# Useless 512-column matmuls in TensorE's waits during the softmax of a one-token GQA decode block

## The chip, the cores and the metric

One core of one Trainium2 chip. The metric is device time of one execution in microseconds (us), the median over several executions. Executions of one kernel scatter here by about 0.2%, so differences under some 1.5 us in single runs mean little, and I then read the trace and not the total.

## The reference, cut to what matters

```python
mod = (_silu(c) @ w_mod).reshape(8, 6, 1, 512)         # sa, ca, ga, sb, cb, gb
h = _layernorm(x) * (1 + ca) + sa                      # x: 8 x 1 x 512
# attention: 8 batches, 32 query heads, 8 KV heads, 8192 keys, head size 128, bf16
q = (h @ wq) ...
p = softmax(q @ k_cache.T * 128 ** -0.5)
x = x + ga * ((p @ v_cache) @ wo)
h = _layernorm(x) * (1 + cb) + sb
x = x + gb * (relu(h @ w1 + b1) ** 2 @ w2 + b2)        # w1: 512 x 1792
```

K and V together are 268 MB, and each byte is used once. The whole kernel reads 284 MB (283.66 on the page, part 3).

## The kernel before

K and V come in 64 units of 4 MiB, each with two KV heads of one batch: for each of the eight batches four units of K, then four of V. A ring of four slots in SBUF holds them. A slot is loaded again as soon as TensorE has read it.

```python
units = [(kv, b, p) for b in range(B) for kv in "kv" for p in range(NP)]   # NP = 4
...
    loaded[n] = dma("sync", s_ring[s], lambda e: e.dma_start(slot(s), src), dep)  # dep: slot released
```

A batch begins with its K phase. TensorE transposes 128 key tiles per unit, 32 at a time, VectorE and ScalarE copy them out of PSUM, and TensorE multiplies them by the queries of all heads. The scores stand in PSUM banks 0 to 3. The softmax follows. It is a chain of small steps that goes back and forth between the engines, and TensorE waits in four places, marked here A to D:

```python
t = op("vector", lambda e: e.tensor_reduce(m1[:], m4[:], AX.X, ALU.max), maxes)
t = op("vector", lambda e: e.tensor_scalar(Dm[:], Qmask[:], m1[:, 0:1], None, ALU.mult), [t, k_all], "vecP")
T_ps = bank(7)[:, 0:4]                                                           # A
t = op("tensor", lambda e: e.matmul(T_ps, R4[:], Dm[:]), [t, stg_free[3]])       # maximum, transposed
t = op("vector", lambda e: e.tensor_reduce(mq[:], T_ps, AX.X, ALU.max), [t])
k_neg = op("vector", lambda e: e.tensor_scalar(negm[:], mq[:], -inv_sqrt, None, ALU.mult), [t])
exps = []                                                                        # B
... # four exponentials on ScalarE; 64 transposes of P on TensorE; copies into Pm
t = op("vector", lambda e: e.tensor_reduce(rs1[:], rs4[:], AX.X, ALU.add))
t = op("vector", lambda e: e.tensor_scalar(rhs_r[:], R4m[:], rs1[:, 0:1], None, ALU.mult), [t, k_all], "vecP")
tot_ps = bank(3)[:, 0:32]                                                        # C
t = op("tensor", lambda e: e.matmul(tot_ps, ONES[:, :], rhs_r[:]), [t])          # row sums
k_rinv = op("vector", lambda e: e.reciprocal(rinv[:], tot_ps), [t], "vecP")      # D
```

The V phase has four units of 32 matmuls with 512 columns each, in four column groups of the array, then a copy, four small matmuls and a scaling by `rinv`. For the last batch this code stands apart. Between its V units it already projects with `wo`, and it loads the last quarter of `wo`, then `w1` and `w2`, behind the last V. A few 128-column fillers of the same kind as in the change (`pe_fill`) stand there already.

## Time and profile before

| what | value | read from |
|---|---|---|
| time | 671.87 us median of 3 (671.45 to 672.91) | the runs |
| busy: TensorE matmul, VectorE, ScalarE | 72%, 45%, 35% of the span | page, part 1 |
| load queue | 98.7% of 16 engines' span | page, part 3 |
| period of a batch | 77.7 us, that is 33.55 MB at 432 GB/s | chain of waits |
| mean granted TensorE clock | 0.862 | span and clock of the core |

The page of the kernel before, parts 2 and 3: TensorE's granted clock, the DMA share (tenths, in 40 slices of 16.8 us), the rate in each slice, then the queue of the loads and the queue that fetches instructions.

```profile
PEclk9999986899859977799868988699757997589979
DMA  9999999999999999999999999999999999999995
GB/s 374 435 419 426 430 431 432 430 430 434 432 432 430 428 436 432 434 430 432 432 430 434 428 432 430 434 434 434 430 426 434 432 436 430 426 436 430 438 393 209
...
q1 hardware_dynamic: 12612, 283.65, 98.7%
q8 instruction: 13, 0.21, 0.1%
```

The DMA row says what bounds the kernel: in every slice but the last the digit is 9, so the DMA engines are busy for 90% or more of it. The rate is 432 GB/s over whole batches; single slices read up to 438. The clock row shows the thing that the change goes after: the clock falls once or twice in every batch, to digits of 5 to 7.

The groups of instructions: the V matmuls (L564). The columns after the bar are busy us, mean ns of one, then TensorE's idle time just before them and what ended most of it.

```profile
L564 PE MATMUL PS<-ring,Pm 128*32 128x512 bf16 x992 | 85.2, 504 | 62.7 <-DMA ring<-in_A_v_cache_dram 58.3
```

TensorE waits 58 us in all for V to arrive (58.3, in 14 waits). In the V phases of the first seven batches it is ahead of the loads.

The timeline of the kernel before, from the softmax of the last batch to the end, TensorE's lines only, with cuts. The columns are start, duration, engine and line, operation, count, and in brackets the idle time before it and its releaser. L511 is the matmul of the maximum, L525 the transposes of P, L544 the row sums, L564 the V units, L645 the last projection by `wo`, L682 the matmuls with `w1`, L699 those with `w2`; L431 are fillers that were there before.

```profile
628.86 0.18 PE L511 MATMUL PS<-Dm,R 128*128 128x4 bf16 x1 [1.26 <-DVE Dm L509]
...
630.29 2.65 PE L525 MATMUL PS<-IDENT,P_sb 128*64 128x128 bf16 x64 [1.25 <-ACT P_sb L516]
...
633.93 0.41 PE L544 MATMUL PS<-rhs_r,ONES 128*128 128x32 f32 x2 [0.99 <-DVE rhs_r L542]
...
634.88 3.02 PE L564 MATMUL PS<-ring,Pm 128*32 128x512 bf16 x32 [0.54 <-DVE rinv L545]
...
638.89 3.59 PE L564 MATMUL PS<-ring,Pm 128*32 128x512 bf16 x32
...
657.77 1.15 PE L645 MATMUL PS<-oTn,wo_sb 128*128 128x64 bf16 x32 [0.29 <-DVE oTn L640]
...
660.68 0.94 PE L431 MATMUL PS<-IDENT 128*128 128x128 bf16 x14
...
661.87 3.55 PE L682 MATMUL PS<-hbT,ring 128*128 128x64 bf16 x56 [0.25 <-DVE hbT L675]
...
665.55 1.48 PE L699 MATMUL PS<-ring,hidT 128*8 128x256 bf16 x24
```

The four waits A to D last 1.26, 1.25, 0.99 and 0.54 us (in the other batches the third is 0.85 or 0.86 and the rest are the same). After them the clock is down (0.50 in the stretch from 636 to 642 us): two V units take 3.02 and 3.59 us, where a warm one takes 1.9 (1.91 in the first batch, at a clock of 1.00). From the first V unit to the start of L645 the trace has no wait of TensorE for a load.

### The profile page before, as it was taken

How to read it: one execution, taken by the hardware profiler on the slowest of the kernel's cores; microseconds unless marked ns; L12 is line 12 of the kernel's file. 1: busy time of each engine (PE TensorE's matmuls, PEld its weight loads, DVE VectorE, ACT ScalarE, POOL GpSimd, SP SyncE). 2: the span in 40 equal slices, each digit the busy share in tenths (PEclk: the TensorE clock that was granted, in tenths of full speed). 3: DMA queues.
4: the chain of work that ended last, by engine and by line, in shares of the span. 5: the costliest groups of instructions: out<-in, count | busy, mean ns of one | idle time of the engine just before them, and what ended most of it. 6: DMA issues, size and time to landing. Idle time of an engine off the chain costs nothing.

```text
span 670.8 us, 15938 instructions
## 1 busy us (share of the span) xinstructions
PE 481.1 (72%) x7366; PEld 345.6 (52%) x7366; DVE 300.3 (45%) x568; ACT 235.3 (35%) x281; POOL 17.0 (3%) x67
## 2 busy tenths in 40 slices
PE   2289843997459964698629973699647986399787
PEld 2277621875137731576318751477316753187445
DVE  2146721567116751466216661267414673166612
ACT  2045600465006630365105650166203661056500
POOL 7200000000000000000000000000000000000000
PEclk9999986899859977799868988699757997589979
DMA  9999999999999999999999999999999999999995
GB/s 374 435 419 426 430 431 432 430 430 434 432 432 430 428 436 432 434 430 432 432 430 434 428 432 430 434 434 434 430 426 434 432 436 430 426 436 430 438 393 209
DMA packets 12682, 283.96 MB, mean 423 GB/s; under 512 B 1234, under 2 KB 2291, under 8 KB 3956
## 3 DMA queue, kind: packets, MB, share of 16 engines
q1 hardware_dynamic: 12612, 283.65, 98.7%
q8 instruction: 13, 0.21, 0.1%
q14 instruction: 9, 0.07, 0.0%
q10 hardware_dynamic: 48, 0.02, 0.0%
HBM read 283.66 MB, written 0.01 MB: 423 GB/s over the span
## 4 chain that ended last, share of the span: by engine, by line
PE 57%; DMA 35%; DVE 4%; ACT 2%; issue 1%
PE PS L439 36%; DMA ring<-in_A_k_cache_dram 33%; PE PS L454 9%; PE PS L564 4%; PE PS L525 3%; DMA ring<-in_w_mod_dram 2%; ACT KTb L444 1%; ACT P_sb L516 1%; DVE m L459 1%; DVE Pm L538 1%; PE PS L544 1%; PE PS L483 1%; PE PS L682 0%; DVE rinv L545 0%; PE PS L386 0%
## 5 line engine op out<-in xcount | busy, mean ns | idle before, releaser
L444 ACT ACTIVATE KTb<-PS 128x1024 bf16<-128x1024 bf16 x192 | 196.7, 1024 | 369.9 <-PE PS L439 369.9
L439 PE MATMUL PS<-IDENT,ring 128*128 128x128 bf16 x4096 | 268.1, 228 | 45.7 <-DMA ring<-in_A_k_cache_dram 36.5
L439 PEld LDWEIGHTS PS<-IDENT,ring 128*128 128x128 bf16 x4096 | 247.5, 103 | 94.0 <-DMA ring<-in_A_k_cache_dram 38.0
L446 DVE COPY KTb<-PS 128x1024 bf16<-128x1024 bf16 x320 | 210.2, 688 | 145.3 <-PE PS L439 143.3
L564 PE MATMUL PS<-ring,Pm 128*32 128x512 bf16 x992 | 85.2, 504 | 62.7 <-DMA ring<-in_A_v_cache_dram 58.3
L573 DVE CAST O_sb<-PS 128x512 bf16<-128x512 f32 x31 | 21.4, 692 | 144.1 <-PE PS L564 144.1
L454 PE MATMUL PS<-KTb,Qb 128*32 128x512 bf16 x1024 | 78.8, 384 | 4.5 <-ACT KTb L444 4.5
L564 PEld LDWEIGHTS PS<-ring,Pm 128*32 128x32 bf16 x992 | 30.1, 118 | 99.4 <-DMA ring<-in_A_v_cache_dram 59.6
L525 PE MATMUL PS<-IDENT,P_sb 128*64 128x128 bf16 x512 | 25.2, 269 | 10.4 <-ACT P_sb L516 10.0
L577 PEld LDWEIGHTS PS<-SEL,O_sb 128*128 128x128 bf16 x124 | 5.2, 98 | 45.5 <-DVE O_sb L573 45.5
L516 ACT ACTIVATE P_sb<-PS,negm 128x512 bf16<-128x512 f32 x32 | 21.6, 686 | 18.9 <-DVE negm L513 18.9
L525 PEld LDWEIGHTS PS<-IDENT,P_sb 128*64 128x64 bf16 x512 | 21.0, 140 | 13.5 <-ACT P_sb L516 13.2
L538 DVE COPY Pm<-PS 64x512 bf16<-64x512 bf16 x48 | 20.1, 421 | 16.2 <-PE PS L525 15.1
L454 PEld LDWEIGHTS PS<-KTb,Qb 128*32 128x32 bf16 x1024 | 15.4, 94 | 21.0 <-ACT KTb L444 8.5
L577 PE MATMUL PS<-SEL,O_sb 128*128 128x8 bf16 x124 | 8.0, 170 | 24.8 <-DVE O_sb L573 24.8
L459 DVE TENSOR_REDUCE m<-PS 128x1 f32<-128x512 f32 x32 | 22.1, 689 | 6.6 <-PE PS L454 6.6
L535 ACT ACTIVATE Pm<-PS 64x512 bf16<-64x512 bf16 x16 | 9.5, 593 | 5.5 <-PE PS L525 5.4
L580 DVE TENSOR_TENSOR oTn<-PS,rinv 128x8 bf16<-128x8 f32 x31 | 6.0, 193 | 10.9 <-PE PS L577 10.9
L398 PE MATMUL PS<-haT,ring 128*128 128x8 bf16 x128 | 3.7, 168 | 9.1 <-DMA ring<-in_A_wq_dram 6.4
L672 ACT ACTIVATE std<-PS,epst 128x8 f32<-128x8 f32 x1 | 0.3, 268 | 26.0 <-PE PS L670 26.0
L544 PE MATMUL PS<-rhs_r,ONES 128*128 128x32 f32 x16 | 4.2, 349 | 7.0 <-DVE rhs_r L542 7.0
L511 PE MATMUL PS<-Dm,R 128*128 128x4 bf16 x8 | 1.4, 178 | 10.1 <-DVE Dm L509 10.1
(114 smaller groups left out, 105.7 us busy)
## 6 DMA issues: line engine op xcount, KB each, us to landing
ring<-in_A_k_cache_dram SPq DMA_DIRECT2D x32, 4096.0 KB, 35.2
ring<-in_A_v_cache_dram SPq DMA_DIRECT2D x31, 4096.0 KB, 27.8
ring<-in_A_wq_dram SPq DMA_DIRECT2D x1, 4096.0 KB, 19.8
ring<-in_w_mod_dram SPq DMA_DIRECT2D x1, 3072.0 KB, 10.5
wo_sb<-in_A_wo_dram SPq DMA_DIRECT2D x1, 3072.0 KB, 45.2
ring<-in_A_v_cache_dram SPq DMA_DIRECT2D x1, 2048.0 KB, 22.4
ring<-in_B_w_dram SPq DMA_DIRECT2D x1, 1536.0 KB, 14.7
ring<-in_B_w_dram SPq DMA_DIRECT2D x1, 1344.0 KB, 21.8
```

Of the source, the lines that this page charges most:

```text
L439: t = op("tensor", lambda e, j=j, i=i: e.matmul(STG[j][:, i, :], src[:, 32 * k + 8 * j + i, :], IDENT[:, :], is_transpose=True), [loaded[n ...
L444: stg_free[j] = op("scalar", lambda e, j=j, dst=dst: e.activation(dst, STG[j], ACT.Copy), [t], "scaP")
L446: stg_free[j] = op("vector", lambda e, j=j, dst=dst: e.tensor_copy(dst, STG[j]), [t], "vecP")
L454: t = op("tensor", lambda e, hf=hf, q=q, rhs=rhs: e.matmul(PS[32 * q:32 * (q + 1), k, :], Qb[:, 2 * p + hf, :], rhs, start=(p == 0 and hf ...
L459: return op("vector", lambda e: e.tensor_reduce(m4[:, k:k + 1], bank(k), AX.X, ALU.max), [t])
L516: exps.append(op("scalar", lambda e, k=k: e.activation(P_sb[:, k, :], bank(k), ACT.Exp, bias=negm[:, 0:1], scale=inv_sqrt, accum_out=rs4[: ...
L525: t = op("tensor", lambda e, k=k, i=i, hf=hf, src=src: e.matmul(STG[k][64 * hf:64 * (hf + 1), i, :], src, IDENT[:, :], is_transpose=True, ...
L538: done.append(op("vector", lambda e, dst=dst, frm=frm: e.tensor_copy(dst, frm), [t, k_pm], "vecP"))
L544: t = op("tensor", lambda e: e.matmul(tot_ps, ONES[:, :], rhs_r[:]), [t])
L564: t = op("tensor", lambda e, p=p, m=m, cg=cg, vt=vt, Obank=Obank: e.matmul(Obank[32 * cg:32 * (cg + 1), :], lhs[:, p, 32 * m:32 * m + 32], ...
L573: t = op("vector", lambda e, osb=osb, Obank=Obank: e.tensor_copy(osb, Obank), [t], "vecP")
L577: t = op("tensor", lambda e, i=i, osb=osb, oT_ps=oT_ps: e.matmul(oT_ps, osb[:, i * 128:(i + 1) * 128], SEL[:, i, :], start=(i == 0), stop= ...
```

## The change

Its intent: fill the four waits with plain matmuls whose results nobody uses, in the hope that TensorE then keeps its clock of 1.00 and runs the V phase of each batch at full speed. The banks written (4 and 1) are free at that moment.

```diff
+        def pe_stream(n, at):
+            rhs = IDENT[:, :].unsqueeze(1).to_broadcast([128, 4, 128])
+            for _ in range(n):
+                op("tensor", lambda e: e.matmul(
+                    bank(at).rearrange("p (a r) -> p a r", a=4), IDENT[:, :], rhs))
...
             t = op("vector", ... Dm ...)
+            pe_stream(5, 4)                      # A
             T_ps = bank(7)[:, 0:4]
...
             k_neg = op("vector", ... negm ...)
+            pe_stream(5, 4)                      # B
             exps = []
...
             t = op("vector", ... rhs_r ...)
+            pe_stream(3, 1)                      # C
             tot_ps = bank(3)[:, 0:32]
             t = op("tensor", lambda e: e.matmul(tot_ps, ONES[:, :], rhs_r[:]), [t])
             k_rinv = op("vector", lambda e: e.reciprocal(rinv[:], tot_ps), [t], "vecP")
+            pe_stream(2, 1)                      # D
```

## The prediction

> **What bounds the kernel now.** The DMA engines. The utilisation slices show DMA at 90% or more in 39 of 40, and the queue table gives the load queue 98.7% of the 16 engines' span. Stretches of 10 us from 20 to 640 move 413 to 442 GB/s, mostly 429 to 436. [...] In the chain of waits the batches repeat every 77.7 us; eight loads of 4 MiB in 77.7 us are 432 GB/s. The K phase of a batch takes TensorE 16 x 2.44 = 39.0 us, as long as four loads. The softmax adds about 8 us, and the V phase, where TensorE is faster than the loads, pays it back: its waits for V loads sum to 58 us, some 7 us a batch. A load lands a median 35.2 (K) or 27.8 (V) us after its issue; alone it would take 9.7, so the queue always holds more work. TensorE's lag never starves DMA.
>
> **What the change does.** It adds 120 matmuls of 512 columns (15 in each of 8 batches), with no new semaphore and no copy; it removes nothing. One such stream costs, estimated from V units of 32 matmuls in groups of four (1.94 us at full clock, 3.59 at half), 0.24 us warm and 0.45 cold. The gaps of TensorE before the four consumers (timeline, waits): 1.26 us before the maximum transpose, 1.25 before the P transposes, about 0.9 before the row-sum matmul, 0.54 before V. Warm fillers take 1.2, 1.2, 0.7 and 0.5: they fit, with 0 to 0.3 us of delay per batch. The clock is still 1.00 when the softmax starts.
>
> What it buys is clock. In the last batch the granted clock is 1.00 up to 634 us and then 0.50 from 636 to 642; the first two V units take 3.02 and 3.59 us instead of 1.94. [...] With fillers both should run near 1.94, at least the first: 1 to 2.7 us off TensorE's chain per batch.
>
> **How much is on the critical path.** In batches 1 to 7 nothing: TensorE arrives earlier at V and waits longer for V. Only after the last softmax is TensorE the last chain. There it gains up to 2.7 us by the second V unit, but loads cut it short: the last piece of wo lands at about 656.4 (needed at 657.8), the main part of w2 at about 664.5 (needed at 665.55). They queue behind a saturated DMA and don't move. So at most about 1 us reaches the end; I count 0.8 us, less a little for fillers in the way and for a new cold spell where TensorE waits for wo.
>
> **Predicted time: 671.2 us, range 669.9 to 672.7.** Faster by over 2%: 1%; within 2%: 98%; slower by over 2%: 1%.
>
> **What would show it right or wrong.** Right: batch period still 77.7 us; DMA slices unchanged; waits of the V matmuls for V loads up by some 5 to 15 us; the first V unit after a softmax at 1.9 to 2.2 us with clock 1.00; TensorE busy up by 20 to 30 us before what warm V saves; P transposes at most 0.3 us later after the last scores. Wrong: a batch period off 77.7, a DMA slice below 90% in the middle, or the last V units still at half clock.
>
> **What would make it wrong.** Fillers running cold (0.45 us each) would delay the softmax by up to 3 us, harmless but in the last batch. A clock drop moved onto the last w1 matmuls (3.4 us warm) would cost up to 3 us. Either stays under 1%.

671.87 us, less the 0.8 us counted at the end, with a little given back for fillers in the way and a new cold spell, is 671.2. The 9.7 us of a load alone is an estimate: 4 MiB at the 432 GB/s of a batch.

## More of the kernel before

A run is called fast or slow by its state. Only the verdicts of repeated runs use that; a single run has the state "unknown".

TensorE runs the eight batches as a loop: its instruction stream exists once and is repeated. The other engines' streams are unrolled.

## The result, and the profile after

| | before | after |
|---|---|---|
| median | 671.71 us (4 runs, 671.45 to 672.91) | 672.50 us (4 runs, 671.75 to 672.71) |
| profiled span | 670.8 us | 670.6 us |
| mean granted clock | 0.862 | 0.885 |

The ratio is 1.0006, with a 95% interval of 0.9989 to 1.0024: the same. A ratio is the mean time of one kernel's fast runs over that of the other's of the same rounds, so it is not quite the ratio of the medians.

The page of the changed kernel, the same lines as above.

```profile
PEclk9997997899869996699859997699967998699996
DMA  9999999999999999999999999999999999999995
GB/s 372 434 419 428 430 432 430 430 432 430 434 432 429 432 434 432 434 426 434 432 432 434 424 432 432 436 436 422 434 432 432 436 430 426 434 432 436 436 389 217
...
q1 hardware_dynamic: 12612, 283.65, 98.8%
q8 instruction: 13, 0.21, 0.1%
```

The DMA rows have not changed. The clock row has; it still falls in each batch, but later, where TensorE waits for V (to 0.50 in the seventh batch, below). The groups, V matmuls and fillers (L436):

```profile
L574 PE MATMUL PS<-ring,Pm 128*32 128x512 bf16 x992 | 81.0, 484 | 63.8 <-DMA ring<-in_A_v_cache_dram 62.9
...
L436 PE MATMUL PS<-IDENT 128*128 128x512 bf16 x120 | 31.3, 380 | 0.0
```

The V matmuls are busy for 4.2 us less, and TensorE waits 4.6 us longer for V. (The 380 ns of one filler come from matmuls that overlap. Five take 1.25 us together.) The two figures don't belong to the same batches. Of the 4.2 us, 3.3 fall in the last batch, whose V units are shown below. In the first seven, V is busy for 75.3 us, against 76.1 before. There the first V units took 6.0 us less in all (13.4 against 19.4), and the third ones took 5.0 us more (23.6 against 18.6). The third unit of the seventh batch in the timeline, before and then after:

```profile
565.70 1.91 PE L564 MATMUL PS<-ring,Pm 128*32 128x512 bf16 x32 [1.11 <-DMA ring<-in_A_v_cache_dram]
```

```profile
565.85 3.36 PE L574 MATMUL PS<-ring,Pm 128*32 128x512 bf16 x32 [3.85 <-DMA ring<-in_A_v_cache_dram]
```

TensorE comes to the third unit earlier and waits for the same load: 25.9 us in the seven batches, against 16.3. Around the end of this longer wait the clock falls (in the seventh batch to 0.50 at about 566.2 us). So the cold spell has moved from the first unit to the third, where the wait for the fourth load takes it up: that wait shrank from 42.0 to 37.0 us.

What the clock did around one softmax: a stretch of the profile from the last scores to the second V unit of the seventh batch. The columns are length, busy us of each engine with instruction counts, then the granted clock, the DMA share and GB/s. First the kernel before:

```profile
545.00:562.00 17.00, 11.66 (x170) 6.80 (x171) 9.09 (x22) 6.35 (x13) 0.00 (x0) 0.80 1.00 432
```

The same stretch of the changed kernel:

```profile
545.00:562.00 17.00, 14.15 (x210) 7.29 (x202) 9.22 (x22) 6.01 (x12) 0.00 (x0) 1.00 1.00 432
```

The clock goes from 0.80 to 1.00, and the loads run at 432 GB/s in both.

The timeline of the changed kernel, the last batch, the lines that answer to those of before (L518 maximum, L533 transposes of P, L574 V, L655 `wo`, L692 `w1`, L709 `w2`):

```profile
628.41 0.18 PE L518 MATMUL PS<-Dm,R 128*128 128x4 bf16 x1
...
629.84 2.64 PE L533 MATMUL PS<-IDENT,P_sb 128*64 128x128 bf16 x64 [0.15 <-ACT P_sb L524]
...
634.43 1.91 PE L574 MATMUL PS<-ring,Pm 128*32 128x512 bf16 x32
...
637.32 1.91 PE L574 MATMUL PS<-ring,Pm 128*32 128x512 bf16 x32
...
656.63 1.86 PE L655 MATMUL PS<-oTn,wo_sb 128*128 128x64 bf16 x32 [2.32 <-DMA wo_sb<-in_A_wo_dram]
...
660.47 1.65 PE L431 MATMUL PS<-IDENT 128*128 128x128 bf16 x14
...
661.91 3.52 PE L692 MATMUL PS<-hbT,ring 128*128 128x64 bf16 x56
...
665.60 1.48 PE L709 MATMUL PS<-ring,hidT 128*8 128x256 bf16 x24 [0.16 <-DVE hidT L700]
```

Both V units now take 1.91 us; the second ends 3.2 us earlier than before (639.2 against 642.5). Then TensorE has to wait 2.32 us for the last piece of `wo`. It starts the projection 1.14 us earlier than before, at 656.63, but at a lower clock: it fell during the wait, and is 0.50 from 655 us until past 662. The projection takes 1.86 us where it took 1.15, and the 14 old fillers 1.65 where they took 0.94. At the first matmul with `w1` the two kernels stand level again, 661.91 against 661.87.

### The profile page after: what moved, and what is told of

Its sections match the earlier page's. It is cut to its first block, busy times and chain, and to the rows that moved or that the text cites. A ratio compares the mean times of both kernels' runs of the same rounds, so it can differ in the third digit from the quotient of the medians.

```text
span 670.6 us, 16178 instructions
## 1 busy us (share of the span) xinstructions
PE 498.8 (74%) x7486; PEld 345.4 (52%) x7486; DVE 299.3 (45%) x568; ACT 235.1 (35%) x281; POOL 17.0 (3%) x67
## 4 chain that ended last, share of the span: by engine, by line
PE 51%; DMA 40%; DVE 5%; ACT 2%; issue 1%; SPq 0%; ACTq 0%
PE PS L445 36%; DMA ring<-in_A_k_cache_dram 35%; PE PS L460 9%; DMA wo_sb<-in_A_wo_dram 4%; DVE Pm L546 3%; PE PS L574 2%; ACT KTb L450 1%; DMA KTb<-in_A_x_dram 1%; ACT P_sb L524 1%; DVE m L465 1%; PE PS L533 1%; PE PS L436 0%; PE PS L692 0%; PE PS L553 0%; PE PS L431 0%
## 5 line engine op out<-in xcount | busy, mean ns | idle before, releaser
L574 PE MATMUL PS<-ring,Pm 128*32 128x512 bf16 x992 | 81.0, 484 | 63.8 <-DMA ring<-in_A_v_cache_dram 62.9
L574 PEld LDWEIGHTS PS<-ring,Pm 128*32 128x32 bf16 x992 | 29.1, 114 | 100.8 <-DMA ring<-in_A_v_cache_dram 64.1
L436 PE MATMUL PS<-IDENT 128*128 128x512 bf16 x120 | 31.3, 380 | 0.0
L587 PEld LDWEIGHTS PS<-SEL,O_sb 128*128 128x128 bf16 x124 | 5.2, 98 | 45.1 <-DVE O_sb L583 45.1
L546 DVE COPY Pm<-PS 64x512 bf16<-64x512 bf16 x48 | 19.5, 419 | 13.4 <-PE PS L533 12.4
L533 PE MATMUL PS<-IDENT,P_sb 128*64 128x128 bf16 x512 | 20.4, 222 | 2.0 <-ACT P_sb L524 1.2
L533 PEld LDWEIGHTS PS<-IDENT,P_sb 128*64 128x64 bf16 x512 | 15.2, 109 | 9.8 <-ACT P_sb L524 9.8
L436 PEld LDWEIGHTS PS<-IDENT 128*128 128x128 bf16 x120 | 9.9, 103 | 10.8 <-issue 3.4
```

What stands on the lines that cost most here:

```text
L436: op("tensor", lambda e: e.matmul(bank(at).rearrange("p (a r) -> p a r", a=4), IDENT[:, :], rhs))
L533: t = op("tensor", lambda e, k=k, i=i, hf=hf, src=src: e.matmul(STG[k][64 * hf:64 * (hf + 1), i, :], src, IDENT[:, :], is_transpose=True, ...
L546: done.append(op("vector", lambda e, dst=dst, frm=frm: e.tensor_copy(dst, frm), [t, k_pm], "vecP"))
L574: t = op("tensor", lambda e, p=p, m=m, cg=cg, vt=vt, Obank=Obank: e.matmul(Obank[32 * cg:32 * (cg + 1), :], lhs[:, p, 32 * m:32 * m + 32], ...
L587: t = op("tensor", lambda e, i=i, osb=osb, oT_ps=oT_ps: e.matmul(oT_ps, osb[:, i * 128:(i + 1) * 128], SEL[:, i, :], start=(i == 0), stop= ...
```

## The experiments

The theory: the loads bind. The fillers keep the clock through the softmax, what they save becomes waiting for V, and at the end waiting for `wo`. The main rival: TensorE's chain binds, and the fillers cost in the softmax what they give back in V, so that the net is zero. A zero result fits both; the experiments must break the tie. Twelve kernels ran, and all passed the comparison with the reference.

### 1. The changed kernel again, and 2. with fillers in the wait for wo

> The changed kernel once more, unaltered, so that the tail variant can be set against it in the same rounds. The theory (loads bind; the fillers' gain is absorbed by waits for V and, at the end, for the last piece of wo) expects 671.5 to 672.7 us and a ratio to before of 0.999 to 1.002. A rival, that the fillers cost time in the softmax which their warm clock pays back, expects the same ratio; this run does not separate them.

```diff
                     t = direct(112, 128, 3, False, True)
+                    pe_stream(9, 7)
                     t = op("vector", ... oTn_p ... rinv_p ...)
```

> The changed kernel with nine more 512-column fillers where TensorE waits 2.3 us for the last piece of wo in the final batch. Theory (the wait for wo cooled the clock, and the cold projection, transposes and fillers then gave back what was left of the gain): the projection by wo still starts near 656.6 us, limited by the load, but takes 1.15 instead of 1.86 us; the first w1 matmul starts near 660.8 instead of 661.9; the w2 matmuls start near 664.5, when w2 lands; span 669.5 to 669.9, about 0.8 to 1.0 us shorter than the changed kernel, a ratio of 0.9985 to it. Rival (the tail is bound by the loads of w1 and w2 alone): no change of the span, first w2 matmul still at 665.6.

Measured in five rounds together with the kernel before (672.26 us): the changed kernel again 672.29 us (671.66 to 672.56, ratio 1.0001, interval 0.9987 to 1.0014), the tail variant 671.72 us (671.44 to 672.52, ratio 0.9997, interval 0.9983 to 1.0011). The tail variant's timeline, from the wait for `wo`:

```profile
654.16 2.11 PE L436 MATMUL PS<-IDENT 128*128 128x512 bf16 x9
...
656.64 1.13 PE L656 MATMUL PS<-oTn,wo_sb 128*128 128x64 bf16 x32 [0.38 <-DMA wo_sb<-in_A_wo_dram]
...
660.73 3.55 PE L693 MATMUL PS<-hbT,ring 128*128 128x64 bf16 x56 [0.25 <-DVE hbT L686]
...
664.71 1.48 PE L710 MATMUL PS<-ring,hidT 128*8 128x256 bf16 x24 [0.43 <-DMA ring<-in_B_w_dram]
```

In this profile each step fell where the theory put it. The projection starts when `wo` lands and takes 1.13 us; `w1` starts at 660.73; then the tail runs into the landing of `w2`, at 664.7. The span was 669.7 us against 670.6, as expected. The totals are 0.6 us apart in the median, and the intervals overlap, so this is no version that is shown to beat both; 0.9 us of 670 is about what one execution differs from the next. The expected ratio of 0.9985 to the changed kernel was missed: the two ratios above make it 0.9996. One reason is to be seen in the repeated run of the changed kernel: there the projection happened to run warm (1.14 us) and only the fillers after it were cold, `w1` started at 661.26, and the span was 670.1 us.

### 3. and 4. More fillers: 25 and 60 instead of 5 in wait A

```diff
-            pe_stream(5, 4)                      # A
+            pe_stream(25, 4)                     # or 60
```

> The changed kernel with 25 instead of 5 fillers before the maximum transpose: 20 more at 0.24 us, so each of the eight softmaxes ends 4.8 us later. Theory (loads bind): batch period still 77.7 us, waits of the V matmuls for V loads down by about 4 us a batch; in the last batch the 4 us of waits for V and wo swallow it: 671.5 to 673 us. Rival (TensorE's chain binds, and gain and cost of the fillers happened to cancel): 8 x 4.8 = 38 us more, about 710 us.

> As the last one with 60 fillers: 13.2 us later in each softmax, 106 us of added TensorE work in all. Theory: batch period still 77.7 us, because TensorE has some 19 us of waiting in a batch and a load issued at the end of a V unit has more than 13 us of others queued ahead; only the last softmax shows, with 13.2 less the 4 us of waits and 1.2 of a cold spell that no longer occurs: about 8.3 us more than the changed kernel, 679.5 to 682 us. Rival (TensorE's chain binds): about 778 us.

With 25: 673.95 us (672.02 to 674.22), ratio 1.0016, interval 1.0000 to 1.0033. The batch period is still 77.7 us, though TensorE has 8 x 4.4 = 35 us more to do (25 fillers took 5.50 us in the chain of waits, so 4.4 us for twenty). The rival's 710 us is out. The waits for V fell from 62.9 to 45.1 us, 2.5 us a batch and not the 4 that I expected; a good part of the rest came out of the third V units, which now started after a short wait or none: they took 14.0 us in the first seven batches, against 23.6. I had expected 671.5 to 673 us. The median is 1 us above that. In the profiled execution (674.22 us) a cold spell fell between the V units of the last batch: its third V unit took 2.94 us instead of 1.91, and the first piece of the fourth 1.90 instead of 1.05.

With 60: 705.63 us. Neither 680 nor 778. The period grew to about 80 us, so the theory as I had put it missed something. The page of that run, the instruction queue:

```profile
q8 instruction: 76, 1.25, 0.7%
```

The instruction queue carried 76 packets instead of 13, and the chain of waits had waits of 1.6 to 4.4 us before the K phases and of 5.8 us before the last V phase, with no releaser but "issue". So two causes were mixed in this run: a late softmax, and instructions fetched again and again. Experiments 5 and 9 to 10 look at each alone. How the 33 us divide between them stays open: the delay of 5 is 8.7 us a softmax, and 55 more fillers at 0.22 us are about 12. From the second batch to the seventh no V unit waited for its load in this run, so TensorE's slack was used up.

### 5. A late softmax without one more instruction on TensorE

The kernel before, with twelve useless reductions on VectorE ahead of wait A.

```diff
+            for _ in range(12):
+                t = op("vector", lambda e: e.tensor_reduce(std2[:, 0:1], bank(0), AX.X, ALU.max), [t])
             t = op("vector", ... Dm ...)
```

> The kernel before, with no fillers, and twelve useless reductions of 0.69 us on VectorE before the mask of each softmax: each softmax ends 8.3 us later, and TensorE gets no instruction more, so that nothing of the 60-filler run's extra instruction fetching can come in. Theory (loads bind, a batch has more TensorE waiting than that, and the queue holds loads for longer): batch period 77.7 us still; only the last softmax shows, for by then no waits are left in the kernel before: 6 to 10 us in all, 678 to 682 us. Rival (every softmax is on the chain): 8 x 8.3 = 66 us, about 738 us. Second rival (the 60-filler run was slow because the delay starved the loads): batch period over 79 us and the slices of the DMA below 90% here as well.

An earlier try of this, without the dependency between the reductions, was a race.

Measured: 682.65 us (680.13 to 682.96), ratio 1.0150, interval 1.0128 to 1.0172. In the chain of waits a reduction took 0.725 us from start to start, so 8.7 us were added to each softmax, 70 us in all; about 10 arrived at the end (11.0 between the medians). The K phases start at these times (chain of waits, first 64 transposes of a batch):

```profile
118.53 5.81 PE PS L439 x64
...
196.24 6.20 PE PS L439 x64
...
273.97 6.56 PE PS L439 x64
...
351.68 5.31 PE PS L439 x64
...
429.39 5.69 PE PS L439 x64
...
507.84 5.72 PE PS L439 x64
...
586.52 5.64 PE PS L439 x64
```

Four periods of 77.7 us, as before, then 78.5 and 78.7. The last K phase of the kernel before (chain of waits):

```profile
585.14 6.59 PE PS L439 x64
```

Seven softmaxes that were 8.7 us late cost 1.4 us at the start of the last K phase (586.52 against 585.14), and the last one cost the rest. This is the proof that the softmax of the first seven batches is not on the chain, and why nothing that is saved there can come out. The slack is nearly used up by then, as the two last periods show. The DMA slices stay at 9 up to the tail, so the second rival, loads starved by the delay, is out at 8.7 us. The median is 0.65 us over the range that I had given; the 1.4 us of the two last periods cover it.

### 6. and 7. The loads taken away: half a slot for each K and V unit

From the fifth unit on only half of a slot is loaded and the other half keeps old data. The result is wrong, though the comparison with the reference did not notice it. The same edit in both kernels:

```diff
-                loaded[n] = dma("sync", s_ring[s], lambda e: e.dma_start(slot(s), src), dep)
+                z = UNIT if n < NSLOT else UNIT // 2
+                loaded[n] = dma("sync", s_ring[s], lambda e: e.dma_start(RING[:, s, 0:z], src[:, 0:z]), dep)
```

> The kernel before with the loads of K and V cut to half a slot from the fifth on (the other half keeps old data; the result is wrong on purpose): the DMA engines have 124 MB less to move and TensorE's chain binds. Theory: batch period down to 60 to 65 us (39.0 for K, 8 for the softmax, 12 to 18 for V), 535 to 580 us in all; the first V units after a softmax still partly at half clock.

> The changed kernel with the same halved loads (wrong on purpose). Theory: here the fillers are worth what they save on TensorE, 1 to 4 us a batch, 8 to 30 us in all, a ratio of 0.95 to 0.985 to the halved kernel before; batch period 58.5 to 59.5 us. Rival (the fillers cost in the softmax what they give back in V): ratio to the halved kernel before 0.995 to 1.005.

Measured, three rounds on the same chip: halved kernel before 557.68 us (555.28 to 558.23; one execution of 568.46 at a clock of 0.927 counts as slow and is left out of the ratio), halved changed kernel 550.98 us (550.72 to 551.05). Ratios to the same runs of the unhalved kernel before are 0.8280 and 0.8201, so the fillers give a ratio of 0.8201 / 0.8280 = 0.990, or 6.7 us between the medians (6.1 if the slow execution is left out of them too). The two intervals, 0.8261 to 0.8299 and 0.8187 to 0.8215, don't overlap. The rival expected 0.995 to 1.005. With the loads out of the way the same fifteen fillers pay. (Of the 7.2 us between the two profiled executions, about 1.5 were there before the first filler: the first matmul of a maximum starts at 82.12 us in the one and at 80.66 in the other.)

They pay less than the 8 to 30 us that I expected. Where it comes from: the V units of the sixth batch in the halved kernel before (timeline),

```profile
394.90 3.60 PE L565 MATMUL PS<-ring,Pm 128*32 128x512 bf16 x32 [0.54 <-DVE rinv L546]
...
399.50 3.60 PE L565 MATMUL PS<-ring,Pm 128*32 128x512 bf16 x32
...
404.11 3.58 PE L565 MATMUL PS<-ring,Pm 128*32 128x512 bf16 x32
```

and in the halved changed kernel:

```profile
395.86 1.91 PE L575 MATMUL PS<-ring,Pm 128*32 128x512 bf16 x32
...
398.75 1.91 PE L575 MATMUL PS<-ring,Pm 128*32 128x512 bf16 x32
...
401.65 1.91 PE L575 MATMUL PS<-ring,Pm 128*32 128x512 bf16 x32
```

In three of the eight batches the halved kernel before ran V units cold; in the other five its V units stayed warm without help (1.87 to 1.94 us each in the chain of waits). And in the halved changed kernel six of the seven later K phases began cold: their first 64 transposes took 5.0 to 5.4 us instead of 3.73. In the halved kernel before only one of the seven did, and its periods without a cold spell, 60.9 to 61.0 us, are shorter than any with fillers. The fillers moved part of the cold spell from V to the next K, and what they gain comes from the batches that they keep from the long cold spells (two periods of 66.05 and 63.99 us without them). The cold K start is 1.6 us of the difference between the period, 61.6 to 61.9 us, and the 58.5 to 59.5 that I expected; another 1.0 us is a wait at the loop's start, which I had not counted. What the fillers do beyond the mean is to make the time steady: four executions within 0.33 us, against 3 us without them, or 13 us if the slow one is counted.

### 8. Transposes as fillers

```diff
-                op("tensor", lambda e: e.matmul(bank(at).rearrange(...), IDENT[:, :], rhs))
+                for a in range(4):
+                    op("tensor", lambda e, a=a: e.matmul(
+                        bankb(at)[:, 128 * a:128 * (a + 1)], IDENT[:, :], IDENT[:, :], is_transpose=True))
```

> The changed kernel with each 512-column filler replaced by four 128-column transposes, the same stream of columns but no plain matmul. If transposes don't count as activity for the clock[...], the clock after a softmax falls as in the kernel before: the stretch from 625 to 640 us has a mean granted clock of about 0.85 and the first V unit of a batch takes 3 us or more in most batches. If they count, the clock is 1.00 there and the unit takes 1.9 to 2.0 us. Time 671 to 674 us either way, since the loads bind.

Measured: 689.66 us in one run. The time is a miss, and it has nothing to do with the clock (experiments 9 and 10). For the clock the run is good. The stretch from the first fillers through the first V unit of the seventh batch, and that unit in the timeline:

```profile
559.00:569.00 10.00, 9.23 (x167) 6.50 (x167) 4.82 (x16) 3.97 (x10) 0.00 (x0) 1.00 1.02 437
```

```profile
566.88 1.91 PE L575 MATMUL PS<-ring,Pm 128*32 128x512 bf16 x32
```

The stretch for the test, 625 to 640 us, no longer fits, because this run is 17 us longer; the stretch above is its equal one batch earlier. In all of the first seven batches the unit took 1.9 us, as with plain matmuls; in the kernel before four of the first seven took 3.23 to 3.58. (In the eighth batch a wait of 6.03 us put down to "issue" stands before the unit, and it is cold, 3.63 us.) In this kernel transposes held the clock as well as matmuls did: 1.00 in the stretch above and in the one of the changed kernel. The K phases of the kernel before show it without any filler: the last one begins at 585.14 us at a clock of 0.50, TensorE does nothing but transposes until 591.66, and from about 591.2 us on, after some 6 us, the clock is 1.00. The "plain" in the change is not what makes it work.

### 9. and 10. Instructions alone: 45 and 20 tiny matmuls where TensorE waits for K

```diff
+                    if not lastb and p == NP - 1:
+                        for _ in range(45):      # or 20
+                            op("tensor", lambda e: e.matmul(bank(7)[:, 0:8], IDENT[:, :], IDENT[:, 0:8]))
```

> The changed kernel with 45 useless matmuls of 8 columns at the end of each V phase but the last, where TensorE waits about 5 us for K anyway: as many instructions more in TensorE's loop as in the run with transposes as fillers (45 matmuls and 45 weight loads), but hardly any time. Theory (the two slow filler runs were slow because TensorE's loop body outgrew what it keeps, and was fetched anew for every batch): instruction queue at 60 to 76 packets instead of 13, waits put down to issue of 2 to 6 us at the loop's branches, 684 to 692 us. Rival (those runs were slow through the extra stream or the transposes): 13 packets and 671.5 to 673 us.

> The same with 20 matmuls, as many instructions as the run with 25 fillers, which still fetched only 13 packets. Theory: 13 packets, 671.5 to 673.5 us. Rival (useless matmuls in this place cost time of themselves): some 4/9 of what the 45 cost.

Measured, one run each: 688.96 us with 45, 671.63 us with 20, beside the kernel before at 671.62. The instruction queue of the run with 45, then of the run with 20:

```profile
q8 instruction: 76, 1.25, 0.7%
```

```profile
q8 instruction: 13, 0.21, 0.1%
```

And two of the eight waits that the chain has in the run with 45 at the loop's branches:

```profile
197.81 4.17 issue
...
647.72 6.36 issue
```

The rival, that such matmuls cost time of themselves in this place, expected 4/9 of the cost with 20 of them; they cost nothing. So the cost is that of instructions, not of their work. Counted from the program, TensorE's loop body has about 850 matmuls in the kernel before, each with a weight load (the page has 7,366 of each): 1,700 instructions. The change makes it 1,730. The runs with 35 added matmuls (25 fillers in A, or 20 tiny ones), 1,770, still fetch 13 packets. Those with 60 (transposes, or 45 tiny ones), 1,820, fetch 67 and 76 (1.10 and 1.25 MB); that with 70 (60 fillers in A), 1,840, fetches 76. The 63 packets more carry 1.04 MB, 16.5 KB each; they are nine for each of the seven K phases with a wait before them (with transposes 54, for six such K phases). What sets the limit is not shown; by these runs it lies between some 1,770 and 1,820 instructions in the loop. Of the 17 us, the last wait is 6.4 us; the rest came as a batch period of 79.3 instead of 77.7 us (from one fourth V unit to the next). How a wait of 4 us at the loop's start becomes 1.5 us of period while the DMA queue still has loads in it I have not settled.

### 11. and 12. Half the change

```diff
             pe_stream(5, 4)    # A            first_two: kept;    last_two: taken out
             pe_stream(5, 4)    # B            first_two: kept;    last_two: taken out
             pe_stream(3, 1)    # C            first_two: taken out;  last_two: kept
             pe_stream(2, 1)    # D            first_two: taken out;  last_two: kept
```

> Only the first two streams of five fillers (before the maximum transpose and before the P transposes). The two waits of 2.5 us in all before the P transposes are the longest quiet stretch; if that is what drops the clock, V's first unit takes 1.9 to 2.0 us in at least six of the eight batches. If the quiet stretch around the row sum matters as much, it takes over 2.5 us in three batches or more. Time 671 to 673 us either way.

> Only the last two streams, three fillers before the row-sum matmul and two before V. If the early quiet stretch is what drops the clock, V's first unit is still over 2.5 us in three batches or more, as in the kernel before (five of eight). If not, 1.9 to 2.0 us in most. Time 671 to 673 us either way.

Measured, one run each: 672.66 us and 671.41 us, the same as the rest. The first V unit was cold in four of eight batches with only A and B filled (3.3 to 3.6 us), and in none with only C and D filled (1.9 us in all eight). I had thought that the long early quiet stretch drops the clock. To fill it was not enough, and to fill the late one was: the row sums and the reciprocal, the last thing before V. For the first V unit the ten fillers in A and B could have been left out. In the profiled run of the kernel before the clock fell to 0.50 during the transposes of P in the first seven batches (stretches of 0.6 us), and in the eighth within the first V unit, at about 635.6 us, though no wait of A to D was longer than 1.26 us. In three of the seven it was back at 1.00 when V began. Why the unit was cold in five of eight batches with the same waits, and not in all, no run here settles. These are single runs, but 0 of 8 against 4 of 8 and 5 of 8 in the kernel before is plain.

## Why the prediction was right

The time, 672.5 us, lies in the range, 0.2 us below its upper end, and the class was right. The class follows from a mechanism that the runs bear out. That the number lies inside is partly luck: the 0.8 us of gain did not come, and the kernel before alone spread from 671.26 to 673.22 us over all rounds. Point by point:

- **The loads bind and the softmax of batches 1 to 7 is off the chain: right.** Period 77.7 us in both kernels, DMA slices unchanged. Shown by experiment 5, where 70 us of added delay cost 10, and from the other side by 6 and 7, where the fillers began to pay when the loads were halved.
- **Fillers fit into the waits: right.** From the start of the last scores to the transposes of P it takes 3.3 us in both traces (626.99 to 630.29, and 626.53 to 629.84). The delay was zero. Five fillers took 1.25 us against the estimated 1.2.
- **First V unit at 1.9 us, clock 1.00: right** in all eight batches of the profiled run (1.91 us, clock 1.00), and at 1.93 or 1.94 us in the seven that the chain of waits shows for the repeated run.
- **TensorE busy up by 20 to 30 us before what warm V saves: right.** It rose from 481.1 to 498.8 us; with the 4.2 us that V saved this is 21.9.
- **Waits for V up by 5 to 15 us: a little high.** They rose by 4.6 us. The wait before the third unit rose by 9.6, as the prediction has it, but the cold spell that it brought to that unit took 5.0 back from the wait before the fourth. The prediction had a new cold spell only at the end, not in the first seven batches; since the loads bind there, it cost nothing.
- **0.8 us gained at the end: wrong in the measured total.** The limits were right: `wo` released TensorE at 656.6 and `w2` at 664.7, and the tail variant reached both. The step that failed is "I count 0.8 us, less a little for fillers in the way and for a new cold spell". The cold spell was not little. It took 0.71 us in the projection and 0.7 in the 14 old fillers, which ate all of the 1.14 us by which the projection started earlier. That the cold spell does it is shown by the profile of experiment 2, which filled the wait and started `w1` 1.18 us earlier; the totals are too close to show it.
- **What I did not see:** that the prediction's mechanism has a second limit, the size of TensorE's loop. Ninety instructions more than the change has cost 17 us (experiment 9).

## What to carry to other kernels

Before you speed up a stage, ask which wait the time would go into: here it was the wait for V, and a check that costs one run (delay the stage on purpose, and see how much comes out at the end) tells it before any tuning. Fillers for the clock did their work here in the last quiet stretch before the matmuls that need the clock (none of eight first V units cold with C and D alone, four of eight with A and B alone), and they were worth something only where TensorE bound (6.7 us with the loads halved, a ratio of 1.0006 with the full loads); then a steadier time was a good part of it. Look where the cold spell goes: here it moved to the next long wait (third V units 23.6 us instead of 18.6). In a looped instruction stream, count instructions as a resource and look at the instruction queue's packets after each addition (here 13 with some 1,770 instructions in the loop, 67 or 76 with 1,820).
